# First MLP on token tiles of 512, 512, 256 and 512 that cross batch ends, in place of four batches of 448

## The chip, the cores and the metric

The kernel runs on one core of one Trainium2 chip. A core has five engines that work side by side, each on its own in-order stream of instructions: TensorE (PE in the profile; its weight loads are listed apart as PEld), VectorE (DVE), ScalarE (ACT), GpSimd (POOL) and SyncE (SP, which here only issues DMAs). The metric is the device time of one execution in microseconds (us), the median of several runs. TensorE's granted clock has two levels, 1.2 and 2.4 GHz; the profile gives it as a share of the upper one.

## The reference

Four batches of 448 tokens go through attention (12 heads of 64, RMS norm on q and k), a ReLU MLP with a LayerNorm and a residual, and a gated MLP whose gate mixes the tokens of a batch. All is fp32.

```python
q_n, k_n = rmsnorm(q, g_q), rmsnorm(k, g_k)                 # (4, 12, 448, 64)
attn = softmax(q_n @ k_n.T / sqrt(64)) @ v
x = attn.transpose(0, 2, 1, 3).reshape(4, 448, 768)
xn = (x - mean(x)) / sqrt(var(x) + 1e-6) * g_ln             # the first MLP
x = x + maximum(xn @ w_ch1, 0) @ w_ch2                      # 768 -> 3072 -> 768
h = maximum(x @ w_in, 0)                                    # the gated MLP, 768 -> 1024
u, v = h[..., :512], h[..., 512:]
v_s = einsum('ts,bsd->btd', w_spatial, layernorm(v)) + b_spatial[None, :, None]
out = (u * v_s) @ w_out                                     # 512 -> 768
```

The first MLP works on each token by itself: nothing in it asks where a batch ends. The attention before it and the gate behind it work batch by batch.

## The kernel before

Activations lie transposed: 128 model or hidden columns on the partitions, tokens along the free axis. Products in the MLPs are done as three matmuls (`THREE`) over parts of the operands, a high part and the remainder (hi and lo), so each activation tile is written twice, once by ACT (hi) and once by DVE (lo).

The first MLP takes the 3072 hidden columns in 24 units `u` of 128. For a unit and a batch `b` there are two groups of 18 matmuls, each 128x128 weights against 448 tokens: `ph` (L663, 6 blocks of the 768 model columns by 3) makes the hidden tile, ACT (L673) and DVE (L678) turn it into `h` hi and lo, and `pm` (L686, 6 output blocks by 3) multiplies by the second weight. DVE adds each of the 6 outputs into the residual `y` (L693). That is 24 x 4 x 36 = 3,456 matmuls of 448 tokens. The group order (`plan_groups`) is `ph` of one (u, b), then `pm` of the one before. `ph` tiles rotate over 2 PSUM banks, so a `ph` group waits until DVE has read the `ph` two groups earlier; `pm` tiles rotate over 3 and 3.

Weights stream in for each unit. DVE converts each piece of them, `wc`, in four operations (L92 to L95), ACT (L101) and POOL (L171) split it into `ws`.

The kernel is a list of steps with a cost, an engine and a due number `n` (`op`), and `arrange` orders each stage's steps greedily by those and emits every engine's stream in that order. Stages that matter here:

- A: attention over 24 pairs of heads, its outputs `x` transposed by PE (`pxT`, L541) and copied into `y` by ACT (L101), one copy per pair; the LayerNorm of batches 0, 1 and 2 as far as `lnx`; the hidden and output groups of unit 0 on batch 0, put in between.
- B, the transition: the rest of units 0 and 1. Beside it run the LayerNorm of batch 3 (a chain of short DVE operations to `lnab`, a broadcast by 8 small PE transposes `pbc`, L590, then on POOL a multiply L618 and an add L621 for each of 6 blocks, `lnx`), the `xn` tiles of batches 2 and 3 (ACT L635, DVE L638, 6 blocks each) and the conversion of the weight pieces for units 1 to 3.
- C: units 2 to 23. Then the gated MLP, batch by batch (`gv` L743, `gu` L806, `gs` L827, `gp` L874). Batch 0 takes its `y` from SBUF; batches 1 to 3 were stored to `y_dram` at the end of C (L1094, three DMAs on ACT's queue) and are loaded again; SP's small loads of the gate's bias `br` (L1124) and of `wout_r` (L1153) stand in the same stage as they.

Of the kernel before, what the change touches and what calls it, by code (L numbers as in the profile page):

```python
# [39 lines left out]
def attention_mlp_gated(ctx, tc, q, k, v, g_q, g_k, g_ln, w1, w2, w_in, w_sp, b_sp, w_out, out):  # L40
# [630 lines left out]
    def h_act(u, b, pl, tag):  # L671
        hs = pl.tile([P, 2, S], F32R, tag=tag, name=f"h{u}_{b}")
        nc.scalar.activation(hs[:, 0, :], hid[u, b][0][:, :S], AF.Relu)  # L673
        hid[u, b].append(hs)

    def h_dve(u, b):
        ph, hs = hid[u, b]
# [4 lines left out]
    def o_pe(u, b, m, pl):
        s2, hs = wsp["w2", u], hid[u, b][1]
        po = bank(pl, f"pm{u}_{b}_{m}")
        for e, (a, c) in enumerate(THREE):
# [3 lines left out]
        hid[u, b, m] = po

    def o_dve(u, b, m):
        po = hid.pop((u, b, m))
        nc.vector.tensor_tensor(y[b][:, m, :], po[:, :S], y[b][:, m, :], op=ALU.add)  # L693

    def plan_hidden(u, b, n, after=()):

        o, w1r = f"{u}_{b}", f"w1_{u}"
        pl, hs = ("s", "h0") if after else ("h", "hs")
# [7 lines left out]
        tiles = lambda: (ap["h0"], "h0") if after else (hpool, "h")  # L706
        op(n, "ACT", 0.424, lambda: h_act(u, b, *tiles()), r=["h" + o], w=["hs" + o], new=hs)
        op(n, "DVE", 0.535, lambda: h_dve(u, b), r=["h" + o], w=["hs" + o])

    def plan_outputs(u, b, n, pls):  # L710

        o = f"{u}_{b}"
# [503 lines left out]
```

## Times and profile before

| | us |
|---|---|
| median of 3 runs | 1281.92 (1281.67 to 1282.04) |
| the profiled execution | 1280.78 |
| its span, first to last instruction | 1278.9 |
| PE busy | 1238.7 (97%) |
| DVE busy | 908.3 (71%) |
| ACT busy | 456.1 (36%) |
| POOL busy | 335.8 (26%) |

The granted clock over the span is 0.996. The span is read in four parts: attention up to about 350 us, the transition B to about 415, units 2 to 23 to 1050, the gated MLP from there. "Busy" counts the time in which an engine has an instruction in work; a wait of an in-order engine appears as idle time in front of the instruction that waited, with the instruction that released it.

### The profile page before, as it was taken

Reading aid. Unit: us, or ns where it says so; the run is one execution under the profiler, and the core shown is the slowest. Engines: PE = TensorE matmul, PEld = TensorE weight load, DVE = VectorE, ACT = ScalarE, POOL = GpSimd, SP = SyncE. Lnnn points to the kernel's source line nnn. Section 1 sums busy time; section 2 is a strip of 40 time slices with the busy share of each in tenths; the row PEclk is TensorE's granted clock in tenths of the full one; section 3 lists DMA queues with packets and bytes.
Section 4 is the critical chain, followed back from the end, with each engine's and each line's share of the span. In section 5 each row is a group of like instructions: output and inputs, shape, how many; then the busy total and the mean of one; then the engine's idle time right before and its main releaser. Section 6 shows DMA issues by size and latency. Waiting matters only on the chain.

```text
span 1278.9 us, 16910 instructions
## 1 busy us (share of the span) xinstructions
PE 1238.7 (97%) x6528; PEld 1018.7 (80%) x6528; DVE 908.3 (71%) x1682; ACT 456.1 (36%) x910; POOL 335.8 (26%) x278
## 2 busy tenths in 40 slices
PE   4999999999899999999999999999999999999998
PEld 2555555555589999999999999999999998889998
DVE  7777787876598898787887888777776577543240
ACT  4777887878341222112222121121111123122212
POOL 5654866615061111111111111111111024221110
PEclk9999999999999999999999999999999999999999
DMA  4212211211021432222222233221110044111103
GB/s 101 73 51 62 62 44 44 76 40 42 10 98 40 132 106 93 91 75 85 89 75 83 87 101 108 77 73 50 50 50 25 1 150 178 44 44 38 50 1 87
DMA packets 50863, 89.01 MB, mean 70 GB/s; under 512 B 3952, under 2 KB 39152, under 8 KB 50016
## 3 DMA queue, kind: packets, MB, share of 16 engines
q1 hardware_dynamic: 50352, 83.82, 21.2%
q10 hardware_dynamic: 432, 4.13, 0.8%
q8 instruction: 51, 0.84, 0.3%
q14 instruction: 28, 0.23, 0.1%
HBM read 73.58 MB, written 14.35 MB: 69 GB/s over the span
## 4 chain that ended last, share of the span: by engine, by line
PE 85%; DVE 7%; ACT 3%; DMA 2%; POOL 2%; issue 1%; SPq 0%; ACTq 0%; DVEq 0%
PE ph L663 27%; PE pm L686 26%; PE po L486 5%; PE t L469 5%; PE s L438 5%; PE gp L874 5%; PE gv L743 4%; PE gu L806 3%; PE gs L827 3%; DVE nmx L444 2%; DMA win_ru<-win_dram 1%; ACT PT L101 1%; ACT P L450 1%; PE px L520 1%; DVE PT L479 1%
## 5 line engine op out<-in xcount | busy, mean ns | idle before, releaser
L693 DVE TENSOR_TENSOR y<-pm,y 128x448 f32<-128x448 f32 x576 | 320.4, 614 | 111.9 <-PE pm L686 111.9
L686 PE MATMUL pm<-h,ws 128*128 128x448 f32 x1728 | 369.4, 368 | 3.3 <-DVE y L693 2.5
L663 PE MATMUL ph<-xn,ws 128*128 128x448 f32 x1728 | 366.1, 365 | 0.0
L686 PEld LDWEIGHTS pm<-h,ws 128*128 128x128 f32 x1728 | 326.2, 189 | 31.5 <-issue 3.5
L663 PEld LDWEIGHTS ph<-xn,ws 128*128 128x128 f32 x1728 | 324.3, 188 | 26.0
L171 POOL TENSOR_TENSOR ws<-wc,ws 128x768 fp32r<-128x768 f32 x48 | 89.5, 1865 | 574.4 <-ACT ws L101 518.4
L673 ACT ACTIVATE h<-ph 128x448 fp32r<-128x448 f32 x96 | 52.1, 542 | 343.3 <-PE ph L663 336.1
L444 DVE TENSOR_REDUCE nmx<-s 112x2 f32<-112x896 f32 x96 | 104.2, 1086 | 43.4 <-PE s L438 42.5
L450 ACT ACTIVATE P<-s,nmx 112x448 f32<-112x448 f32 x192 | 121.3, 640 | 19.8 <-DVE nmx L444 16.3
L469 PEld LDWEIGHTS t<-ident,P 112*112 112x112 f32 x768 | 74.3, 133 | 42.3 <-ACT PT L101 20.5
L469 PE MATMUL t<-ident,P 112*112 112x112 f32 x768 | 92.8, 264 | 12.0 <-ACT PT L101 7.0
L438 PE MATMUL s<-kT,qT 64*112 64x448 f32 x384 | 98.0, 589 | 2.7 <-ACT P L450 1.9
L91 ACT ACTIVATE wc<-wr 128x768 f32<-128x768 f32 (+1 forms) x64 | 54.7, 859 | 85.7 <-DMA win_dram<-wc 42.4
L101 ACT ACTIVATE ws<-wc 128x768 fp32r<-128x768 f32 x48 | 40.6, 846 | 111.9 <-DVE wc L95 57.4
L486 PE MATMUL po<-PT,vr 112*64 112x448 f32 x384 | 79.2, 555 | 0.0
L101 ACT ACTIVATE PT<-t 112x896 f32<-112x896 f32 x72 | 65.9, 916 | 19.1 <-PE t L469 18.9
L678 DVE SCALAR_TENSOR_TENSOR h<-ph,h 128x448 fp32r<-128x448 f32 x96 | 59.2, 617 | 14.4 <-ACT h L673 14.4
L743 PE MATMUL gv<-winv,ys 128*112 128x512 f32 x288 | 67.2, 392 | 0.0
L743 PEld LDWEIGHTS gv<-winv,ys 128*112 128x112 f32 x288 | 50.1, 174 | 15.8
L94 DVE SCALAR_TENSOR_TENSOR wc<-wr,wc 128x768 int32<-128x768 int32 (+1 forms) x64 | 59.7, 935 | 1.5
L95 DVE SCALAR_TENSOR_TENSOR wc<-wr,wc 128x768 uint32<-128x768 uint32 (+1 forms) x64 | 60.0, 951 | 0.5
L874 PE MATMUL gp<-wout,gg 128*128 128x384 f32 x336 | 58.6, 334 | 0.0
(165 smaller groups left out, 1195.7 us busy)
## 6 DMA issues: line engine op xcount, KB each, us to landing
wr<-in_moe_w_ch_dram SPq DMA_DIRECT2D x48, 768.0 KB, 4.5
wr<-in_moe_w_in_dram SPq DMA_DIRECT2D x12, 512.0 KB, 3.7
vr<-in_v_dram SPq DMA_DIRECT2D x24, 224.0 KB, 2.7
kr<-in_k_dram SPq DMA_DIRECT2D x11, 448.0 KB, 4.0
qr<-in_q_dram SPq DMA_DIRECT2D x11, 448.0 KB, 4.7
y_dram<-y ACTq DMA_DIRECT2D x3, 1344.0 KB, 9.3
yl<-y_dram SPq DMA_DIRECT2D x3, 1344.0 KB, 5.6
win_dram<-wc SPq DMA_DIRECT2D x12, 256.0 KB, 5.5
```

Of the source, the lines that this page charges most:

```text
L101: nc.scalar.activation(d, s, AF.Copy)
L171: nc.gpsimd.tensor_tensor(t[:, 1], pl["c"], f32(t[:, 0]), op=ALU.subtract)
L438: nc.tensor.matmul(p[:CP, j, :S], pr["qT"][rows, c * CP : (c + 1) * CP], pr["kT"][rows], start=True, stop=True)
L444: nc.vector.tensor_reduce(t, pr["s", c][:CP, :, :S], axis=AX.X, op=ALU.max, negate=True)
L450: nc.scalar.activation(t, pr["s", c][:CP, j, :S], AF.Exp, bias=pr["m", c][:, j : j + 1], scale=1.0, accum_out=pr["sum"][:, j, c : c + 1],)
L469: nc.tensor.transpose(p[:CP, e, c * CP : (c + 1) * CP], pr["P", j, c][:, kc * CP : (kc + 1) * CP], ident[:CP, :CP])
L486: nc.tensor.matmul(pr["po"][j * D : (j + 1) * D, :S], raw["v", i][:, j, kc, :], pr["PT", kc // 2, j][:, kc % 2], start=(kc == 0), stop=(kc ...
L663: nc.tensor.matmul(hid[u, b][0][:, :S], s1[:, a, kk, :], xn[b][:, c, kk, :], start=(kk == 0 and m == 0), stop=(kk == NK - 1 and m == 2),)
L686: nc.tensor.matmul(po[:, :S], s2[:, a, m * P : (m + 1) * P], hs[:, c, :], start=(e == 0), stop=(e == 2))
L693: nc.vector.tensor_tensor(y[b][:, m, :], po[:, :S], y[b][:, m, :], op=ALU.add)
L743: nc.tensor.matmul(pv[:CP, :], ys[b][:, a, kk, c * CP : (c + 1) * CP], W["v", kk][:, e], start=(kk == 0 and m == 0), stop=(kk == NK - 1 an ...
L874: nc.tensor.matmul(po[:, :half_n], gt[g][:, a, i * P : (i + 1) * P], W["out", g][:, e, half * half_n : (half + 1) * half_n], start=(g == 0 ...
```

## The change

The tokens of all four batches, 1792 in a row, are cut into tiles of 512, 512, 256 and 512. `y`, `xn` and the groups of the first MLP go by tile `t` (a group is named by unit, tile and first column), so a unit has the same 144 matmuls on tiles of four sizes. What is made by batch is written in pieces: `pieces_of(b)` gives one piece for batch 0 (tile 0, 448 tokens), two for batch 1 (64 of tile 0, 384 of tile 1), three for batch 2 (128 of tile 1, 256 of tile 2, 64 of tile 3), one for batch 3 (448 of tile 3). The copies into `y`, the multiply of `lnx` and both parts of `xn` are done piece by piece: 18 more of each.

In the transition tile 1 of unit 0 is done in two groups, the 384 tokens of batch 1 early and the 128 of batch 2 late, so there are 3,456 + 36 matmuls in all. The planner's costs follow the number of tokens. The pools `OT` and `x` of the attention have one buffer in place of two, `y_dram` is laid out by model column and stored by tile (tile 0 gives its last 64 tokens), and two tiles of the gated MLP lie in other pools.

```diff
-    y_dram = dram.tile([B, P, NK, S], F32, name="y_dram")
+    y_dram = dram.tile([P, NK, B * S], F32, name="y_dram")
...
+    TILES = ((0, 512), (512, 512), (1024, 256), (1280, 512))
+    SEGMENTS = tuple((t, 0, size) for t, (first, size) in enumerate(TILES))
+
+    def pieces_of(b):
+
+        parts = []
+        for t, (first, size) in enumerate(TILES):
+            lo, hi = max(first, b * S), min(first + size, (b + 1) * S)
+            if lo < hi:
+                parts.append((t, slice(lo - first, hi - first), slice(lo - b * S, hi - b * S)))
+        return parts
+
+    def batches_of(t, lo, hi):
+        first = TILES[t][0]
+        return range((first + lo) // S, (first + hi - 1) // S + 1)
...
+            for t, cols, own in pieces_of(b):
+                if t not in y:
+                    y[t] = y_a.tile([P, NK, TILES[t][1]], F32, tag=f"y{t}", name=f"y{t}")
+                act_copy(y[t][:, hp, cols], pr["pxT"][:, own])
...
-                nc.gpsimd.tensor_tensor(t, y[b][:, m], ln["bc"][:, 0], op=ALU.mult)
+                for e, cols, own in pieces_of(b):
+                    nc.gpsimd.tensor_tensor(t[:, own], y[e][:, m, cols], ln["bc"][:, 0, own], op=ALU.mult)
...
-    def plan_xn(b, xn_pool, n, step):
+    def plan_xn(b, n, step):
...
-                xn[b] = xn_pool.tile([P, 2, NK, S], F32R, tag="xn", name=f"xn{b}")
-            nc.scalar.activation(xn[b][:, 0, m, :], ln["x", m], AF.Copy, scale=gl_c[:, m : m + 1])
+            for t, cols, own in pieces_of(b):
+                if t not in xn:
+                    tag = "xn" if t < 2 else f"xn{t}"
+                    xn[t] = xn_pools[t].tile([P, 2, NK, TILES[t][1]], F32R, tag=tag, name=f"xn{t}")
+                nc.scalar.activation(xn[t][:, 0, m, cols], ln["x", m][:, own], AF.Copy, scale=gl_c[:, m : m + 1])
...
+            for t, cols, own in pieces_of(b):
+                nc.vector.scalar_tensor_tensor(
+                    xn[t][:, 1, m, cols], ln["x", m][:, own], gl_c[:, m : m + 1], f32(xn[t][:, 0, m, cols]),
+                    op0=ALU.mult, op1=ALU.subtract,
+                )
...
+        o, w1r, k = f"{u}_{t}_{lo}", f"w1_{u}", (hi - lo + 40) / 488
+        pl, hs = ("s", "PT") if after else ("h", "hs")
...
+            xr = [f"xn{b}_{m}" for b in batches_of(*s) for m in kks]
             op(
-                n, "PE", 0.56 * step, lambda kks=kks: h_pe(u, b, kks, pl),
-                r=[w1r, *after] + [f"xn{b}_{m}" for m in kks], w=["h" + o], new=None if kk else pl,
+                n, "PE", 0.61 * k * step, lambda kks=kks: h_pe(u, s, kks, pl),
+                r=[w1r, *after] + xr, w=["h" + o], new=None if kk else pl,
...
-            ("qkT", 2), ("P", 14), ("PT", 5), ("OT", 2), ("x", 2),
+            ("qkT", 2), ("P", 14), ("PT", 5), ("OT", 1), ("x", 1),
...
-        plan_hidden(0, 0, n + 4, ["done"])
+        plan_hidden(0, SEGMENTS[0], n + 4, ["done"])
...
-        plan_xn(2, xn_c, 0, 3)
+        plan_xn(2, 0, 3)
         plan_norm_x(3, 0, 3)
-        plan_xn(3, xn_c, 16, 3)
-        plan_groups(((0, 1), (1, 0), (1, 1), (0, 2), (1, 2), (0, 3), (1, 3)), 0)
+        plan_xn(3, 16, 3)
+        early, late = (1, 0, 2 * S - TILES[1][0]), (1, 2 * S - TILES[1][0], TILES[1][1])
+        s0, s1, s2, s3 = SEGMENTS
+        plan_groups(((0, early), (1, s0), (1, s1), (0, late), (0, s2), (1, s2), (0, s3), (1, s3)), 0)
...
-            plan_groups([(u, b) for b in range(B)], n)
+            plan_groups([(u, s) for s in SEGMENTS], n)
...
-        for b in range(1, B):
+        plan_ys(0, lambda: y[0][:, :, :S], 14, 1)
+        for t, (first, size) in enumerate(TILES):
+            cols = slice(0 if t else S, size)
             op(
-                7 * b + 14, "SPA", 0.6, lambda b=b: nc.scalar.dma_start(y_dram[b], y[b]),
-                r=[f"y{b}_{m}" for m in range(NK)], w=[f"yd{b}"],
+                7 * t + 14, "SPA", 0.6,
+                lambda t=t, cols=cols, first=first: nc.scalar.dma_start(
+                    y_dram[:, :, first + cols.start : first + cols.stop], y[t][:, :, cols]
+                ),
+                r=[f"y{b}_{t}_{m}" for b in batches_of(*SEGMENTS[t]) if b or t for m in range(NK)], w=[f"yd{t}"],
...
-        gp = {"vs": xn_b}
-
-        for nm, n in (("g", 4), ("o", 2), ("u", 4), ("t", 2), ("w", 1), ("vr", 4), ("small", 2)):
+        gp = {}
+
+        for nm, n in (("g", 4), ("o", 2), ("u", 4), ("t", 2), ("vs", 1), ("vr", 4), ("small", 2)):
...
-            nc.sync.dma_start(yl[b], y_dram[b])
+            nc.sync.dma_start(yl[b], y_dram[:, :, b * S : (b + 1) * S])
```

How that moves the streams is seen best in the transition. On PE, before, the broadcast of batch 3's LayerNorm (`pbc3`) stands behind unit 1's hidden group on batch 1 (`ph1_1`); the suffixes are unit, batch, and for `pm` the output block.

```order
L663 MATMUL ph1_0_4053<-xn0_1639,ws2_4010 128x448 x18
...
L663 MATMUL ph1_1_4119<-xn1_2591,ws2_4010 128x448 x18
L590 MATMUL pbc3_0_4150<-ident_63,lnab3_4037 128x112 x4
...
L686 MATMUL pm1_0_0_4166<-h1_0_4091,ws3_4141 128x448 x3
...
L686 MATMUL pm1_1_0_4205<-h1_1_4156,ws3_4141 128x448 x3
...
L663 MATMUL ph0_2_4248<-xn2_4040,ws0_3564 128x448 x18
```

After it, PE's stream at that place; suffixes are unit, tile, first column, and for `pm` the output block.

```order
L689 MATMUL ph1_0_0_4110<-xn0_1637,ws2_4054 128x512 x18
...
L610 MATMUL pbc3_0_4191<-ident_63,lnab3_4081 128x112 x4
...
L715 MATMUL pm1_0_0_0_4205<-h1_0_0_4156,ws3_4175 128x512 x3
...
L689 MATMUL ph1_1_0_4273<-xn1_2603,ws2_4054 128x512 x18
L689 MATMUL ph0_1_384_4307<-xn1_2603,ws0_3607 128x128 x18
L689 MATMUL ph0_2_0_4338<-xn2_4085,ws0_3607 128x256 x18
...
L715 MATMUL pm1_1_0_0_4360<-h1_1_0_4328,ws3_4175 128x512 x3
```

The broadcast now stands ahead of unit 1's hidden group on the second tile, and that group, which takes 128 tokens of batch 2, behind the output group `pm1_0`; the three tiles that follow have 512, 128 and 256 tokens.

On DVE, before, one operation per block writes `xn` of batch 2 (`lnx2_5` is its sixth and last block), and only unit 0's group on batch 2 needs it; `xn3` is batch 3's, `wc5` a weight piece.

```order
L693 TENSOR_TENSOR y0_576<-pm1_0_5_4198,y0_576 128x448
L92 TENSOR_SCALAR wc5_4177<-wc5_4177 128x768
L638 SCALAR_TENSOR_TENSOR xn2_4040<-lnx2_5_3603,gl_c_70,xn2_4040 128x448
L93 TENSOR_SCALAR wc5_4177<-wc5_4177 128x768
L638 SCALAR_TENSOR_TENSOR xn3_4218<-lnx3_0_4179,gl_c_70,xn3_4218 128x448
```

After it, DVE's stream from the pieces of the fifth block to those of the sixth (the three pieces of the fourth stand right ahead).

```order
L92 TENSOR_SCALAR wc4_4146<-wc4_4146 128x512
L662 SCALAR_TENSOR_TENSOR xn1_2603<-lnx2_4_3603,gl_c_70,xn1_2603 128x128
L662 SCALAR_TENSOR_TENSOR xn2_4085<-lnx2_4_3603,gl_c_70,xn2_4085 128x256
L662 SCALAR_TENSOR_TENSOR xn3_4087<-lnx2_4_3603,gl_c_70,xn3_4087 128x64
L93 TENSOR_SCALAR wc4_4146<-wc4_4146 128x512
L723 TENSOR_TENSOR y0_573<-pm1_0_0_0_4205,y0_573 128x512
L94 SCALAR_TENSOR_TENSOR wc4_4146<-wr4_4101,wc4_4146 128x512
...
L723 TENSOR_TENSOR y0_573<-pm1_0_0_5_4243,y0_573 128x512
L92 TENSOR_SCALAR wc5_4222<-wc5_4222 128x768
L662 SCALAR_TENSOR_TENSOR xn1_2603<-lnx2_5_3646,gl_c_70,xn1_2603 128x128
```

The last piece that unit 1's group on tile 1 reads, `xn1` of block 5, now stands behind the conversion of `wc4`, six adds and the first step of `wc5`, all in the one stream.

## Rows read from the trace of the kernel before

**Rows 1.** The page, part 1: busy time, share of the span, instructions.

```profile
PE 1238.7 (97%) x6528; PEld 1018.7 (80%) x6528; DVE 908.3 (71%) x1682; ACT 456.1 (36%) x910; POOL 335.8 (26%) x278
```

**Rows 2.** Windows: stretch, length, busy PE, PEld, DVE, ACT, POOL, clock, DMA share, GB/s.

```profile
0.00:350.00 350.00, 317.62 (x1982) 174.09 (x1983) 261.55 (x563) 250.45 (x578) 176.82 (x182) 1.00 0.21 55
...
380.00:395.00 15.00, 12.25 (x47) 10.43 (x46) 15.00 (x26) 2.39 (x4) 5.07 (x3) 0.77 0.11 35
...
500.00:600.00 100.00, 100.00 (x495) 92.67 (x494) 79.09 (x139) 22.05 (x32) 12.94 (x7) 1.00 0.27 88
```

**Rows 3.** Timeline of PE, steady units: start, us, line, operation [idle before <-releaser].

```profile
503.02 3.81 PE L686 MATMUL pm<-h,ws 128*128 128x448 f32 x18
...
524.91 3.81 PE L686 MATMUL pm<-h,ws 128*128 128x448 f32 x18
```

**Rows 4.** Timeline of PE in the gated MLP.

```profile
1094.46 16.71 PE L743 MATMUL gv<-winv,ys 128*112 128x512 f32 x72
1111.01 14.56 PE L806 MATMUL gu<-ys,winu 128*128 128x448 f32 x72
1125.41 9.87 PE L827 MATMUL gs<-wsp_s,gvs 112*128 112x448 f32 x48
...
1166.13 29.31 PE L874 MATMUL gp<-wout,gg 128*128 128x384 f32 x168
```

**Rows 5.** Groups by form: line, engine, operation, count, busy us, mean ns, idle before.

```profile
L101 ACT ACTIVATE PT<-t 112x896 f32<-112x896 f32 x72 | 65.9, 916 | 19.1 <-PE t L469 18.9
...
L874 PEld LDWEIGHTS gp<-wout,gg 128*128 128x128 f32 x336 | 58.3, 188 | 0.1
...
L101 ACT ACTIVATE OT<-po 128x448 f32<-128x448 f32 x24 | 13.0, 543 | 31.2 <-PE po L486 31.2
```

**Rows 6.** Timeline of PE in the transition.

```profile
349.60 7.68 PE L663 MATMUL ph<-xn,ws 128*128 128x448 f32 x36
...
360.83 3.88 PE L663 MATMUL ph<-xn,ws 128*128 128x448 f32 x18
364.55 0.93 PE L590 MATMUL pbc<-ident,lnab 112*128 112x112 f32 x8
...
372.86 7.60 PE L663 MATMUL ph<-xn,ws 128*128 128x448 f32 x36
382.95 0.71 PE L686 MATMUL pm<-h,ws 128*128 128x448 f32 x1 [2.49 <-DVE y L693]
383.92 9.82 PE L686 MATMUL pm<-h,ws 128*128 128x448 f32 x35 [0.26 <-DVE h L678]
...
400.88 3.81 PE L686 MATMUL pm<-h,ws 128*128 128x448 f32 x18
```

**Rows 7.** Timeline of DVE in the transition.

```profile
357.45 0.96 DVE L94 SCALAR_TENSOR_TENSOR wc<-wr,wc 128x768 int32<-128x768 int32 x1
...
359.93 0.15 DVE L583 SCALAR_TENSOR_TENSOR lnab<-lnmv,lnab 112x4 f32<-112x4 f32 x1
360.00 3.27 DVE L693 TENSOR_TENSOR y<-pm,y 128x448 f32<-128x448 f32 x6
...
371.66 1.08 DVE L92 TENSOR_SCALAR wc<-wc 128x768 f32<-128x768 f32 x1
...
377.07 1.90 DVE L94 SCALAR_TENSOR_TENSOR wc<-wr,wc 128x768 int32<-128x768 int32 x1
...
382.19 1.14 DVE L693 TENSOR_TENSOR y<-pm,y 128x448 f32<-128x448 f32 x2
```

**Rows 8.** Timeline of POOL in the same stretch.

```profile
379.95 3.32 POOL L621 TENSOR_TENSOR lnx<-lnx,lnbc 128x448 f32<-128x448 f32 x2
```

**Rows 9.** Timeline of PE in the attention: small matmuls with a weight load each.

```profile
152.21 0.98 PE L469 MATMUL t<-ident,P 112*112 112x112 f32 x8 [0.18 <-ACT PT L101]
153.03 0.55 PE L541 MATMUL pxT<-ident,x 112*128 112x112 f32 x4
```

**Rows 10.** The stores of `y`, L1094: time from issue to landing.

```profile
DMA to landing us min/median/max: 6.7/9.3/10.7
```

More of the change, by code (lines that the diff above doesn't have):

```diff
@@ L557, in plan_pair @@
         op(m + 1, "PE", 0.38, xT_pe, r=[f"x{i}"], w=[f"pxT{i}"], new="x")
-        op(m + 1, "ACT", 0.55, xT_act, r=[f"pxT{i}"], w=[f"y{b}_{hp}"])
+        w = [f"y{b}_{t}_{hp}" for t, _, _ in pieces_of(b)]
+        op(m + 1, "ACT", 0.3 + 0.25 * len(w), xT_act, r=[f"pxT{i}"], w=w)
     lnst = {}
@@ L669, in h_pe, with h_act, h_dve, o_pe @@
                 )
[L671 to L677, printed above, removed]
+    def h_act(u, s, pl, tag):
+        t, lo, hi = s
+        hs = pl.tile([P, 2, 512], F32R, tag=tag, name=f"h{u}_{t}_{lo}")
+        nc.scalar.activation(hs[:, 0, : hi - lo], hid[u, s][0][:, : hi - lo], AF.Relu)
+        hid[u, s].append(hs)
+    def h_dve(u, s):
+        n = s[2] - s[1]
+        ph, hs = hid[u, s]
         nc.vector.scalar_tensor_tensor(
-            hs[:, 1, :], ph[:, :S], 0.0, f32(hs[:, 0, :]), op0=ALU.max, op1=ALU.subtract
+            hs[:, 1, :n], ph[:, :n], 0.0, f32(hs[:, 0, :n]), op0=ALU.max, op1=ALU.subtract
         )
-    def o_pe(u, b, m, pl):
-        s2, hs = wsp["w2", u], hid[u, b][1]
-        po = bank(pl, f"pm{u}_{b}_{m}")
+    def o_pe(u, s, m, pl):
+        t, lo, hi = s
+        s2, hs = wsp["w2", u], hid[u, s][1]
+        po = bank(pl, f"pm{u}_{t}_{lo}_{m}")
         for e, (a, c) in enumerate(THREE):
             nc.tensor.matmul(
-                po[:, :S], s2[:, a, m * P : (m + 1) * P], hs[:, c, :], start=(e == 0), stop=(e == 2)
+                po[:, : hi - lo], s2[:, a, m * P : (m + 1) * P], hs[:, c, : hi - lo], start=(e == 0), stop=(e == 2)
             )
[L689 to L698, printed above, removed]
+        hid[u, s, m] = po
+    def o_dve(u, s, m):
+        t, lo, hi = s
+        po = hid.pop((u, s, m))
+        nc.vector.tensor_tensor(y[t][:, m, lo:hi], po[:, : hi - lo], y[t][:, m, lo:hi], op=ALU.add)
+    def plan_hidden(u, s, n, after=()):
+        t, lo, hi = s
+        o, w1r, k = f"{u}_{t}_{lo}", f"w1_{u}", (hi - lo + 40) / 488
+        pl, hs = ("s", "PT") if after else ("h", "hs")
         step = 1 if after else NK
@@ L701, in plan_hidden, with plan_outputs @@
             kks = range(kk, kk + step)
+            xr = [f"xn{b}_{m}" for b in batches_of(*s) for m in kks]
             op(
-                n, "PE", 0.56 * step, lambda kks=kks: h_pe(u, b, kks, pl),
-                r=[w1r, *after] + [f"xn{b}_{m}" for m in kks], w=["h" + o], new=None if kk else pl,
-            )
[L706 to L712, printed above, removed]
+                n, "PE", 0.61 * k * step, lambda kks=kks: h_pe(u, s, kks, pl),
+                r=[w1r, *after] + xr, w=["h" + o], new=None if kk else pl,
+            )
+        tiles = lambda: (ap["PT"], "PT") if after else (hpool, "h")
+        op(n, "ACT", 0.54 * k, lambda: h_act(u, s, *tiles()), r=["h" + o], w=["hs" + o], new=hs)
+        op(n, "DVE", 0.6 * k, lambda: h_dve(u, s), r=["h" + o], w=["hs" + o])
+    def plan_outputs(u, s, n, pls):
+        t, lo, hi = s
+        o, k = f"{u}_{t}_{lo}", (hi - lo + 40) / 488
         for m in range(NK):
             pl = pls[m]
-            op(n, "PE", 0.56, lambda m=m, pl=pl: o_pe(u, b, m, pl), r=["hs" + o, f"w2_{u}"], w=[f"po{o}_{m}"], new=pl)
-            op(n, "DVE", 0.535, lambda m=m: o_dve(u, b, m), r=[f"po{o}_{m}"], w=[f"y{b}_{m}"])
+            op(n, "PE", 0.61 * k, lambda m=m, pl=pl: o_pe(u, s, m, pl), r=["hs" + o, f"w2_{u}"], w=[f"po{o}_{m}"], new=pl)
+            w = [f"y{b}_{t}_{m}" for b in batches_of(*s)]
+            op(n, "DVE", 0.6 * k, lambda m=m: o_dve(u, s, m), r=[f"po{o}_{m}"], w=w)
     def plan_groups(groups, n):
-        for u, b in groups:
-            plan_hidden(u, b, n)
+        for u, s in groups:
+            plan_hidden(u, s, n)
             if todo[0]:
                 plan_outputs(*todo[0], n, "ooommm")
-            todo[0] = (u, b)
+            todo[0] = (u, s)
             n += 7
@@ L1155, in wout_hi @@
         def wout_hi(g):
-            W["out", g] = gp["w"].tile([P, 2, DM], F32R, name=f"wout{g}")
+            if g == 0:
+                W["out"] = xn_b.tile([P, NG, 2, DM], F32R, tag="xn", name="wout")
+            W["out", g] = W["out"][:, g]
             nc.vector.tensor_copy(W["out", g][:, 0], st["wr", g])
```

39 lines of the change are left out of this document (16 added, 23 removed).

## The prediction, written before the changed kernel ran

> **What bounds the kernel now.** I read the page's busy times first: PE works 1238.7 us of the span, 97%, DVE 71% [rows 1]. The windows then show where the missing 3% lies. From 500 to 600 us PE is busy throughout and DVE 79% [rows 2], so the steady units cost what their matmuls cost. A timeline of PE there gives that price: from the first to the last `pm` shown lie six groups of 18, 21.89 us or 202.7 ns a matmul [rows 3]. At 2.4 GHz, the upper level, 448 columns are 186.7 ns; 16.0 ns come on top. The transition is the other place: in 380 to 395 us PE was busy 12.25 of 15 us, DVE all 15, and the clock was 0.77 [rows 2]. PE's timeline shows the stop: 2.49 us before 382.95, for DVE's adds [rows 6].
>
> From 349.60, the first hidden group behind the attention, to 400.88, the output group of unit 0 on its last batch, are 51.28 us [rows 6]. The work in it is 12 groups of 18 at 3.65 us and 0.93 for the broadcast, 44.7. So 6.6 us were lost there: the stop, and matmuls at the lower clock behind it (35 of them took from 383.92 for 9.82 us, where 7.1 would do).
>
> **The change part by part.** All sums stand against the profiled execution's 1280.78 us; the median shown is 1.1 above it, added at the end.
>
> *Steady groups.* The columns are the same; a unit's groups of 448 become 512, 512, 256, 512. If a matmul costs columns/2.4 + 16.0 ns, 144 matmuls of a unit cost the same in both. Other rows give the extra as 13.3 ns (`gu`, 448 columns, 14.40 us for 72), 14.5 (`gp`, 384, 29.31 for 168), 16.5 (`gv`, 512, 16.55 for 72) [rows 4], and 20.0 (3.72 us for the 18 at 360.83) [rows 6]. 0, with bounds 3,492 x (-2.7) = -9.4 and 3,492 x 4.0 = +14.0. DVE adds of 448 come every 0.53 us (six in 3.27, the next at once) [rows 7]; for all sizes together the columns are the same, so DVE's 79% stays.
>
> *The split of tile 1 in unit 0.* 36 more matmuls. Of 128 columns each would cost 53 + 16 = 69 ns, but the nearest small ones, 112 columns with a weight load each, come every 0.10 us (8 in 0.82) [rows 9]. Merged, the 128 columns would cost 53 ns: 36 x 47 ns = +1.7, with bounds 0.6 (16 ns each) and 5.4 (a full 202.7 ns each). Here a rule of the Trainium skill speaks against the change. The rows show weight loads of 188 ns [rows 5] below matmuls that come every 174.5 ns [rows 4], so load and matmul run side by side. "TensorE: Matmul & The Clock Gate", section "The mechanism", says that loads overlap matmuls in flight only when the row group differs; and section "LDWEIGHTS (loading the stationary operand)" prices 128 columns at 107 ns. By that the 36 would cost, as an estimate, 36 x (107 + 16) = 4.4 us. The trace disagrees with the first, and I stay with 1.7.
>
> *The transition.* I follow PE's new order at 2.4 GHz and 16 ns: 18 matmuls are 3.2 us for 384 columns, 4.1 for 512, 2.2 for 256, 1.8 for the late 128. From 349.60: `ph0` early to 352.8, `ph1` on tile 0 to 356.9, `pm0` early to 360.1. The broadcast now stands here, where DVE's short chain has only just ended (359.93 before [rows 7], some 0.6 later with six more pieces of `xn` in it at about 0.1): 0.6 us lost. It is done at 361.6, `pm1` on tile 0 at 365.7, and the group `ph1` on tile 1 runs to its 17th matmul, 369.4. That one needs the last `xn1` piece, which now stands behind the six adds of `pm1`.
>
> When does DVE get there? Its adds of `pm0` begin at about 360.7 and end at 363.5 (six of 0.47). Then 12 operations with both operands in SBUF: six pieces of `xn`, the steps of `wc4` and the first of `wc5`, and the piece itself. Alone, with 0.96 for the 768 columns of L94 [rows 7] and less for fewer, they are about 4.4 us, and six adds of 512 are 3.7: 371.6, a wait of 2.2. But POOL's 12 operations for batch 3's `lnx` begin as soon as the broadcast is through, some 362.5, where before they began with it at 365; they take 1.66 us each here [rows 8], to 382. And beside them DVE's operations grow: L94 is 0.96 without and 1.90 with POOL [rows 7], 0.94 more, and the seven operations from 371.66 to 382.19 took 10.53 us, 1.50 each [rows 7]. I take the 0.94 for the eight that stand in one run and none for the four between adds: 379.1, a wait of 9.7 us. If all 12 pay, 3.8 more.
>
> What a small piece pays is the second place for a rule. The row has a long operation that pays 0.94. The Trainium skill, "SBUF — State Buffer", "Who interferes with whom", calls the port that DVE and GpSimd share an exclusive lock, held for a whole instruction. By it a piece of 64 columns waits as long as one of 448, as I have it. If instead the two shared bandwidth, each operation would grow by its own length (1.90/0.96), the eight by 2.3 us in place of 7.5, and the total below would be 5.2 lower. No row has a small operation beside POOL; the seven rows at 1.50 for lengths from 0.5 to 0.96 fit the lock better.
>
> From 379.1 PE finishes `ph1` (0.5) and runs the late 128 columns (1.8). Then `ph0` on tile 2 needs the bank of `ph1`, which DVE frees only by `h1` on tile 1, ten operations on: 5.9 us alone, 0.6 for `h1` itself, two more waits on POOL: 387.5. That is 6.1 us lost, and the lower clock behind the stop falls mostly within it (the 0.77 of 15 us before is 6.9 us at 1.2 GHz, rest included [rows 2]); 0.4 for the rest. New losses 0.6 + 9.7 + 6.1 + 0.4 = 16.8; the old 6.6 go: **+10.2**. Bounds: -6.6 with no stop at all, and +14.0 with all 12.
>
> *Tile 0 in the attention.* Its unit 0 group has 64 tokens more there and the transition 64 fewer: 0. Attention's own additions are 18 copies and 6 pieces of `xn` on ACT; by OT at 448 elements and PT at 896 [rows 5] a copy's fixed part is 2 x 543 - 916 = 170 ns, so 4.1 us of ACT, which is busy 250 of 350 us [rows 2]. Idle time of ACT covers them where PE does not wait on it; +1, bounds 0 and 4.1. The single buffers of `OT` and `x` cost nothing: the next pair's use is one pair, 350/24 = 14.6 us, later.
>
> *The gate's start.* The last store of `y` took up to 10.7 us to land [rows 10], and SP's loads of the bias and `wout_r` come behind it. It carries 512 tokens in place of 448: 12.2, so 1.5 late, and runs are shorter. DVE and `gs` come behind these loads: +1, bounds 0 and 3.
>
> Sum: 0 + 1.7 + 10.2 + 0 + 1 + 1 = 13.9, 1294.7 profiled, **1296** as the median.
>
> **The rivals.**
> 1. *The pieces come in time* and there is no stop (the other side). The place is the last `xn1` piece; it decides if DVE reaches it by 369.4, which it misses by 2.2 us even without POOL, or if the wait is short enough that the clock stays up. For: the adds read PSUM and may not wait for POOL, and the order leaves POOL's first operations waiting for `lnx` buffers. Against: DVE was full from 365 to 395. Then -6.6 + 1.7 + 2 = -2.9: 1279.0.
> 2. *The extra per matmul falls* to the 13.3 of `gu`, as fewer groups change hands at 512: 13.9 - 9.4 = +4.5, 1286. For: the rows differ by form. Against: `gv`, with 512 columns, has 16.5.
> 3. *It rises* to the 20.0 of the transition: +27.9, 1310.
> 4. *256 columns are bound by the weight load.* Loads of 188 ns [rows 5] under matmuls of 123: if a load overlaps no more than one matmul, 24 x 36 matmuls cost 65 ns more each, +56: 1352. For: loads stay at 188 in rows where the matmul is shorter. Against: small matmuls with loads every 0.10 us [rows 9]. The rule on overlap named above would also end on this side.
>
> **How the numbers follow.** Forecast 0.54, its own range 1286 to 1306 (bounds of the transition's waits, the split and the ends); rival 1 0.20, rival 2 0.13, rival 3 0.06, rival 4 0.07. The range of 1278 to 1309 leaves out the lower third of rival 1, half of rival 3 and rival 4. A measurement of this kernel can tell 0.2%, 2.6 us, from no change: faster is below 1279.4, slower above 1284.5. Rival 1 lies at the first edge: 0.13 faster, 0.05 same, and with a little from rival 2 the chances are 0.15, 0.10 and 0.75.
>
> **What the profile would show.** Matmuls of 512, 256 and 128 columns every 229, 123 and 100 ns in the steady units and the late group; before `ph1`'s last matmuls in the transition an idle time of some 10 us with releaser DVE `xn`, and before `ph0` on tile 2 a second; the clock well below 1 in 370 to 395; pieces of `xn` on DVE of 1 us and more. I am wrong if PE runs through there, or if 256 columns take much over 123 ns.

## The result, and the profile after

The changed kernel takes 1292.38 us (median of 16 runs, 1289.07 to 1295.73), the one before 1281.8 (16 runs, 1279.02 to 1293.38): a ratio on record of 1.0057, 95% interval 1.003 to 1.0084 (the two medians alone stand at 1.0083). It is slower, by 10.6 us of median, at 1296 forecast. The runs before lie in two groups, twelve at 1279 to 1283 us and four at 1291 to 1293.4; the last section has what sets them apart. The profiled execution before (1280.78) is of the lower group, the one after took 1293.51.

The page after, its first part and the clock in 40 slices; these lines answer to [rows 1].

```profile
span 1291.5 us, 17103 instructions
PE 1238.0 (96%) x6564; PEld 967.8 (75%) x6564; DVE 926.5 (72%) x1707; ACT 460.0 (36%) x947; POOL 334.9 (26%) x296
...
PEclk9999999999987999999999999999999999999999
```

PE is busy as long as before, and the clock falls in the 12th and 13th slice, 355 to 420 us. Cut at the same amounts of work left, the two spans are:

| stretch | before, us | after, us | difference | forecast |
|---|---|---|---|---|
| to the first transposes of `k` | 13.02 | 14.03 | +1.0 | 0 |
| attention, to the first `ph` of the transition | 336.58 | 342.00 | +5.4 | +1 |
| from there, until the columns of 22 units are left | 58.57 | 73.56 | +15.0 | +11.9 |
| those 22 units, to the first `gv` | 642.05 | 635.01 | -7.0 | 0 |
| the gated MLP | 228.70 | 226.88 | -1.8 | +1 |
| span | 1278.9 | 1291.5 | +12.6 | +13.9 |

The transition after has 110,592 columns of matmuls, the one before 112,896: tile 0 takes 64 tokens more of unit 0 into the attention. At 2.4 GHz these 2,304 columns are 1.0 us, so for the same work the transition lost 16.0 us and the attention 4.4.

PE's timeline in the transition after (start, length, operation, idle before and its releaser); before it is [rows 6].

```profile
356.03 7.46 PE L689 MATMUL ph<-xn,ws 128*128 128x384 f32 x36
363.32 3.31 PE L715 MATMUL pm<-h,ws 128*128 128x384 f32 x18
367.88 0.60 PE L610 MATMUL pbc<-ident,lnab 112*128 112x112 f32 x4 [1.25 <-DVE y L723]
369.92 0.60 PE L610 MATMUL pbc<-ident,lnab 112*128 112x112 f32 x4 [1.43 <-DVE y L723]
370.28 5.97 PE L715 MATMUL pm<-h,ws 128*128 128x512 f32 x18
376.09 3.79 PE L689 MATMUL ph<-xn,ws 128*128 128x512 f32 x16
385.36 4.95 PE L689 MATMUL ph<-xn,ws 128*128 128x512 f32 x20 [5.48 <-DVE xn L662]
395.93 4.21 PE L689 MATMUL ph<-xn,ws 128*128 128x256 f32 x18 [5.62 <-DVE h L706]
399.94 6.93 PE L715 MATMUL pm<-h,ws 128*128 128x512 f32 x36
...
421.43 4.24 PE L715 MATMUL pm<-h,ws 128*128 128x512 f32 x18
```

The group on tile 1 stops behind its 16th matmul, for an `xn` piece, and tile 2's group stops for `h`, which frees its bank. The broadcast waits twice as well, for the adds that free its banks; the second of these waits is for an add that stands behind the last step of the LayerNorm chain, `lnab`. Four stops are 13.8 us. Windows of the same stretch (busy PE, PEld, DVE, ACT, POOL, then the clock):

```profile
380.00:395.00 15.00, 4.95 (x20) 4.57 (x20) 15.00 (x20) 3.53 (x6) 7.01 (x5) 0.65 0.33 104
386.00:400.00 14.00, 8.38 (x39) 8.10 (x38) 12.69 (x14) 3.53 (x6) 6.55 (x4) 0.50 0.18 63
395.00:410.00 15.00, 14.07 (x82) 13.17 (x83) 10.78 (x23) 0.77 (x2) 0.00 (x0) 0.79 0.04 11
```

PE works a third of 380 to 395 us, DVE all of it, and the clock is still low behind it. DVE's timeline there, as [rows 7] before:

```profile
367.75 1.64 DVE L603 SCALAR_TENSOR_TENSOR lnab<-lnmv,lnab 112x4 f32<-112x4 f32 x1
...
371.64 3.57 DVE L662 SCALAR_TENSOR_TENSOR xn<-lnx,gl_c,xn 128x128 fp32r<-128x128 f32 x3
375.14 0.41 DVE L92 TENSOR_SCALAR wc<-wc 128x512 f32<-128x512 f32 x1
375.47 3.63 DVE L662 SCALAR_TENSOR_TENSOR xn<-lnx,gl_c,xn 128x128 fp32r<-128x128 f32 x3
379.02 0.42 DVE L93 TENSOR_SCALAR wc<-wc 128x512 int32<-128x512 int32 x1
...
384.97 0.93 DVE L662 SCALAR_TENSOR_TENSOR xn<-lnx,gl_c,xn 128x128 fp32r<-128x128 f32 x3
```

Three pieces (128, 256 and 64 tokens) take 3.57 us while GpSimd works on `lnx`, and 0.93 us at 384.97, when it is idle (it waits from 380.4 to 386). One by one, the pieces of 64, 128 and 256 tokens take 1.18, 1.19 and 1.36 us beside GpSimd and 0.27, 0.34 and 0.47 alone: 0.9 us more each, whatever the length. `lnab`, four columns wide, took 1.64 us beside GpSimd's

```profile
367.57 1.80 POOL L189 TENSOR_TENSOR ws<-wc,ws 128x768 fp32r<-128x768 f32 x1 [8.08 <-ACT ws L101]
```

where before it took 0.15 [rows 7]. The adds, which read PSUM, do not wait: 0.68 us for 512 columns at 379.36 with GpSimd at work, 0.67 at 382.71 with GpSimd idle. The steady units, as [rows 3]:

```profile
510.38 2.32 PE L715 MATMUL pm<-h,ws 128*128 128x256 f32 x18
512.53 4.27 PE L689 MATMUL ph<-xn,ws 128*128 128x512 f32 x18
516.63 4.24 PE L715 MATMUL pm<-h,ws 128*128 128x512 f32 x18
520.72 4.24 PE L689 MATMUL ph<-xn,ws 128*128 128x512 f32 x18
...
528.88 2.31 PE L689 MATMUL ph<-xn,ws 128*128 128x256 f32 x18
531.03 4.27 PE L715 MATMUL pm<-h,ws 128*128 128x512 f32 x18
```

A matmul of 512 columns costs 4.09/18 = 227 ns, 13 over columns/2.4, one of 256 costs 2.15/18 = 119, again 13 over; the 448 before had 16.0 over. The group of 512 right behind one of 256 takes a little more: 228.2 ns a matmul over the units, the other two 226.7, so 512 columns cost 227.2 in the mean.

### The profile page after: what moved, and what is told of

Read it like the earlier page. It is cut to its first block, busy times and chain, and to the rows that moved or that the text cites. A ratio compares the mean times of both kernels' runs of the same rounds, so it can differ in the third digit from the quotient of the medians.

```text
span 1291.5 us, 17103 instructions
## 1 busy us (share of the span) xinstructions
PE 1238.0 (96%) x6564; PEld 967.8 (75%) x6564; DVE 926.5 (72%) x1707; ACT 460.0 (36%) x947; POOL 334.9 (26%) x296
## 4 chain that ended last, share of the span: by engine, by line
PE 82%; DVE 9%; ACT 4%; DMA 2%; issue 1%; POOL 0%; SPq 0%; ACTq 0%; DVEq 0%; POOLq 0%
PE pm L715 24%; PE ph L689 23%; PE po L504 6%; PE t L487 5%; PE gv L777 5%; PE s L456 5%; PE gp L908 5%; PE gu L840 4%; PE gs L861 3%; DVE y L723 2%; ACT PT L101 2%; DVE nmx L462 1%; ACT P L468 1%; DVE xn L662 1%; DVE wc L94 1%
## 5 line engine op out<-in xcount | busy, mean ns | idle before, releaser
L723 DVE TENSOR_TENSOR y<-pm,y 128x512 f32<-128x512 f32 (+2 forms) x582 | 324.5, 610 | 97.5 <-PE pm L715 97.0
L689 PE MATMUL ph<-xn,ws 128*128 128x512 f32 (+3 forms) x1746 | 367.4, 365 | 11.1 <-DVE h L706 5.6
L715 PE MATMUL pm<-h,ws 128*128 128x512 f32 (+3 forms) x1746 | 365.8, 363 | 0.7 <-DVE PT L497 0.5
L689 PEld LDWEIGHTS ph<-xn,ws 128*128 128x128 f32 x1746 | 302.0, 192 | 62.0 <-DVE xn L662 5.9
L715 PEld LDWEIGHTS pm<-h,ws 128*128 128x128 f32 x1746 | 300.0, 190 | 52.9 <-issue 1.2
L700 ACT ACTIVATE h<-ph 128x512 fp32r<-128x512 f32 (+2 forms) x97 | 52.0, 536 | 232.9 <-PE ph L689 232.6
L706 DVE SCALAR_TENSOR_TENSOR h<-ph,h 128x512 fp32r<-128x512 f32 (+2 forms) x97 | 59.2, 611 | 14.4 <-ACT h L700 14.4
L92 DVE TENSOR_SCALAR wc<-wc 128x768 f32<-128x768 f32 (+1 forms) x64 | 42.9, 671 | 31.6 <-ACT wc L91 31.5
L95 DVE SCALAR_TENSOR_TENSOR wc<-wr,wc 128x768 uint32<-128x768 uint32 (+1 forms) x64 | 64.1, 1007 | 0.3
```

Of the source, the lines that this page charges most:

```text
L689: nc.tensor.matmul(hid[u, s][0][:, : hi - lo], s1[:, a, kk, :], xn[t][:, c, kk, lo:hi], start=(kk == 0 and m == 0), stop=(kk == NK - 1 and ...
L715: nc.tensor.matmul(po[:, : hi - lo], s2[:, a, m * P : (m + 1) * P], hs[:, c, : hi - lo], start=(e == 0), stop=(e == 2))
L723: nc.vector.tensor_tensor(y[t][:, m, lo:hi], po[:, : hi - lo], y[t][:, m, lo:hi], op=ALU.add)
```

## The experiments

Theory: the transition is lost to DVE operations that have all their operands in SBUF, each of which waits for a whole GpSimd operation, with PE's next operand or bank behind them in DVE's one stream. (The texts put down ahead of the runs speak of two SBUF operands. But the conversion step L93, which reads one, also took 1.50 us beside GpSimd in the kernel before, at 374.15, and 0.56 alone.) Rivals: DVE simply has too much work of its own there; or the loss lies elsewhere (buffers, layout). The steady gain and the attention's loss were open. Ratios are to the kernel before, run on the same chip, both of its groups together; the medians of the lower group alone are 1280.0 to 1280.8 us there. In each case "attention" and "transition" are the stretches of the table above.

**One buffer for OT and x, in the kernel before.**

```diff
-            ("qkT", 2), ("P", 14), ("PT", 5), ("OT", 2), ("x", 2),
+            ("qkT", 2), ("P", 14), ("PT", 5), ("OT", 1), ("x", 1),
...
```

(The planner's count of these buffers goes down with them.)

> The kernel before, with one buffer in place of two for the attention's OT and x tiles and nothing else. In the changed kernel the first hidden group of the transition starts at 356.03 us in place of 349.60, 6.4 later. Theory 'buffers': PE waits for tiles that are still being read, so here that group starts at 353 to 356 and the whole is 1285 to 1288. Rival 'pieces' (the cut copies into y, the cut xn pieces and the wider group of unit 0 shift the order in the attention): start within 1.5 us of 349.6, whole 1281 to 1283. Everything behind the attention keeps its length in both.

1280.05 us, ratio 1.0011 (0.9968 to 1.0053). The attention stretch is 335.3 us, the transition starts at 348.14. 'Buffers' is refuted.

**Four tiles of 448 in the changed kernel.**

```diff
-    TILES = ((0, 512), (512, 512), (1024, 256), (1280, 512))
+    TILES = ((0, 448), (448, 448), (896, 448), (1344, 448))
...
-        plan_groups(((0, early), (1, s0), (1, s1), (0, late), (0, s2), (1, s2), (0, s3), (1, s3)), 0)
+        plan_groups(((0, s1), (1, s0), (1, s1), (0, s2), (1, s2), (0, s3), (1, s3)), 0)
...
```

> The changed kernel with four tiles of 448 (no pieces, no split of tile 1), but with its pools, its planner costs and its layout of y_dram; the xn tile of batch 1 has a stride of 512 columns, the other xn tiles and the hidden tiles 448. Attention: 'buffers' says that the transition starts at 353 to 356, 'pieces' 349 to 351. Transition: 51 to 53 us to unit 0's output group on the last batch, as before, in place of 65, in every theory. Steady units: 'size' (448 columns cost 16.0 ns over columns/2.4, 512 and 256 cost 13.3) says 202.7 ns a matmul in all groups; 'stride' says 200.0 in the hidden groups of batch 1 and 202.7 in the rest; 'schedule' (the new costs and pools do it) says 200.0 everywhere. Whole: 1281 to 1283 with 'pieces' and 'size', 1285 to 1288 with 'buffers' and 'size', 8 less with 'schedule'.

1283.73 us, ratio 1.0044 (1.0001 to 1.0088). Attention 337.1, so neither the pools nor the matmul groups' new costs make it long (nothing is written in pieces here, so the costs of pieces are not tried); transition 59.4. The steady units are a surprise; PE's timeline of its profiled execution:

```profile
701.29 3.88 PE L715 MATMUL pm<-h,ws 128*128 128x448 f32 x18
705.01 3.88 PE L689 MATMUL ph<-xn,ws 128*128 128x448 f32 x18
708.73 3.88 PE L715 MATMUL pm<-h,ws 128*128 128x448 f32 x18
```

3.72 us a group, 206.7 ns a matmul, 20.0 over, in every group of that execution, the tile with the wider stride included. 'Stride' and 'schedule' fall. 'Size' had the price lower, at 202.7: 448 columns cost more than 16.0 over here, in the same groups that had 16.0 in the kernel before.

**Batch 3's LayerNorm later, in the changed kernel.**

```diff
-        plan_ln(3, 0, "o")
+        plan_ln(3, 12, "o")
...
-        plan_norm_x(3, 0, 3)
-        plan_xn(3, 16, 3)
+        plan_norm_x(3, 20, 3)
+        plan_xn(3, 24, 3)
```

> The changed kernel with the LayerNorm of batch 3 planned later, so that its broadcast stands behind unit 1's hidden group on tile 1 and GpSimd's twelve lnx operations begin behind the xn pieces that this group needs. Theory 'lock' (each DVE operation with two SBUF operands waits for a whole GpSimd operation beside it): a piece takes 0.31 us in place of 1.17, the eight DVE operations ahead of pm1's adds take 2.5 us in place of 7.7, and PE's stop inside that group falls from 5.5 us to under 1; some of it comes back as a later wait for xn3, whole 1282 to 1288. Rival 'DVE's own work' (there are simply too many operations ahead): pieces stay near 1 us each, the stop stays at 4 to 6, whole 1291 to 1294.

1282.26 us, ratio 0.9984 (0.9948 to 1.002). Tile 1's group on PE, the pieces of block 5 on DVE that it waits for, and GpSimd, which begins `lnx` only at 385.12:

```profile
377.46 4.25 PE L689 MATMUL ph<-xn,ws 128*128 128x512 f32 x18
```
```profile
378.88 0.94 DVE L662 SCALAR_TENSOR_TENSOR xn<-lnx,gl_c,xn 128x128 fp32r<-128x128 f32 x3
```
```profile
385.12 3.67 POOL L639 TENSOR_TENSOR lnx<-y,lnbc 128x448 f32<-128x448 f32 x2
```

Same instructions, GpSimd away: the three pieces take 0.94 us and the stop of 5.48 is gone. 'Lock' holds, "DVE's own work" does not. Other stops came (2.25, 1.17, 1.59 us), and the transition took 64.5, 9.1 less than in the changed kernel.

**Tile 1's pieces first**, with costs by size for the pieces.

```diff
-        plan_xn(2, 0, 3)
+        plan_xn(2, 0, 0, (1,))
+        plan_xn(2, 8, 1, (2, 3))
...
+            us = sum(0.15 + 0.0012 * (own.stop - own.start) for _, _, own in pieces())
...
```

> The changed kernel with batch 2's xn pieces for tile 1 (six of 128 tokens) planned ahead of its pieces for tiles 2 and 3, and unit 1's hidden group on tile 1 then ahead of the broadcast. Theory (the stop comes from one late piece in DVE's stream, and the stops and the half clock behind them are what the transition lost): no stop in that group, the transition takes 50 to 55 us in place of 65, the whole is 1279 to 1284, about as long as before. Rival (the same DVE work is due in the same stretch, so the wait only moves to the groups on tiles 2 and 3): transition 60 to 65, whole 1288 to 1292.

1277.92 us, ratio 0.9962 (0.9932 to 0.9992), 2.1 us under the median of the lower group: as fast as forecast by the theory and a little more. But the transition took 61.5, not the theory's 50 to 55: that is the rival's number (60 to 65), and the wait did in part move to the next group. What is left, on PE:

```profile
364.16 4.28 PE L694 MATMUL ph<-xn,ws 128*128 128x512 f32 x18
...
373.44 2.12 PE L694 MATMUL ph<-xn,ws 128*128 128x128 f32 x18
381.55 5.94 PE L720 MATMUL pm<-h,ws 128*128 128x512 f32 x18 [5.98 <-DVE y L728]
```

Tile 1's group runs through; the next stop is for adds, which need no GpSimd but stand in DVE's stream behind eight operations beside it, six pieces and two conversion steps, from 370.00 to 380.22. The attention is 340.0 here, 2.0 shorter than in the changed kernel, and nothing else in the edit touches that stage but the corrected costs; the three kernels below that have them take 339.7 to 339.9.

**The pieces alone, in the kernel before** (every line that writes `y`, `lnx` or `xn` of a batch does so in slices).

```diff
+    CUTS = ((0, 448), (0, 64, 448), (0, 128, 384, 448), (0, 448))
...
-            act_copy(y[b][:, hp, :], pr["pxT"][:, :S])
+            for own in cuts(b):
+                act_copy(y[b][:, hp, own], pr["pxT"][:, own])
...
```

> The kernel before with four tiles of 448 as they were, and only the writing in pieces added: the copies into y, the multiply of lnx and both parts of xn are cut at 64 of 448 for batch 1 and at 128 and 384 for batch 2, 18 more instructions of each kind; sizes of matmuls, order and costs stay. From the first transposes of q and k to the first hidden group of the transition the kernel before takes 336.6 us, the changed one 342.0, the one with four tiles of 448 337.1. Theory 'pieces': the cut operations alone make that stretch 340 to 342. Rival 'width' (the group of 512 in the attention and the order that it gives): 336.5 to 337.5. In the transition, 'lock' says that only the pieces of batch 2's last two blocks meet GpSimd, four more operations of 0.9 us, so 58.6 becomes 60 to 63; if pieces cost only their own length there, 58.5 to 59.5.

1284.52 us, ratio 1.0008 (0.9967 to 1.0049). The attention is 339.5 us, 2.9 of the 5.4: between the two expectations, so both have a part. The transition is 58.8, the number of the side that gave pieces their own length only; 'lock' had 60 to 63. The pieces beside GpSimd do take three times as long, as the row shows, but what that cost PE is small: it stopped 2.63 and 0.60 us for the adds behind them, where before it stopped 2.49 and 0.26 [rows 6].

```profile
368.22 2.77 DVE L647 SCALAR_TENSOR_TENSOR xn<-lnx,gl_c,xn 128x128 fp32r<-128x128 f32 x3
```

**All pieces of batch 2 ahead.**

```diff
-        plan_xn(2, 0, 0, (1,))
-        plan_xn(2, 8, 1, (2, 3))
+        plan_xn(2, -2, 0, (1,))
+        plan_xn(2, -1, 0, (2, 3))
```

> As the kernel that writes batch 2's pieces for tile 1 first, but its pieces for tiles 2 and 3 follow at once too, ahead of the LayerNorm chain of batch 3, so that all 18 run before GpSimd begins with lnx. There the stop of 5.98 us was for y adds that stood behind eight pieces beside GpSimd. Theory: pieces take 0.3 us each, that stop falls to 0 to 2 us, the transition takes 55 to 59 us in place of 61.5, the whole is 1272 to 1276. Rival (the later wc and xn3 operations pay the same waits, in the same stretch): 60 to 62, whole 1277 to 1279.

A miss on both sides: 1291.2 us, ratio 1.0039 (1.0005 to 1.0073), transition 75.3. The pieces took 0.3 us each, but PE made three long stops for `h`, the operation that frees a `ph` bank:

```profile
363.92 6.40 PE L694 MATMUL ph<-xn,ws 128*128 128x512 f32 x18 [4.62 <-DVE h L711]
...
386.44 4.21 PE L694 MATMUL ph<-xn,ws 128*128 128x256 f32 x18 [4.01 <-DVE h L711]
...
396.90 8.01 PE L720 MATMUL pm<-h,ws 128*128 128x512 f32 x29 [5.83 <-DVE h L711]
```

The new order runs unit 0's late group at once, which takes the second `ph` bank, and sets `h` behind the pieces, a weight conversion and, later, operations beside GpSimd. The pieces were short here and the stops long: what stands ahead of the bank-freeing operation counts, not the pieces as such.

**Three other sizes.**

```diff
-    TILES = ((0, 512), (512, 512), (1024, 256), (1280, 512))
+    TILES = ((0, 480), (480, 480), (960, 448), (1408, 384))
...
```

> The changed kernel with tiles of 480, 480, 448 and 384 tokens, to read the price of a matmul by its columns in the steady units. In four traces 448 columns cost 202.7 ns (twice) or 206.7 ns (twice), over the whole first MLP of a run, 512 and 256 always 226.7 and 119.4. 'Size': 448 again has 202.7 or 206.7, and 480 and 384 have extras of their own between 13.3 and 20. 'Rest of 512' (only sizes that divide a bank evenly are free of it): 480, 448 and 384 all have 16 or 20 over columns/2.4. 'Length of the matmul' (the extra comes where a matmul is about as long as its weight load of 188 ns): 480 (200 ns) and 384 (160 ns) have 13.3, 448 (187 ns) alone has 16 or 20. Whole: 1290 to 1305, the transition being laid out worse.

1300.98 us (two runs), ratio 1.0111 (1.0026 to 1.0196). The steady groups, twice:

```profile
505.25 3.81 PE L715 MATMUL pm<-h,ws 128*128 128x448 f32 x18
508.90 4.08 PE L689 MATMUL ph<-xn,ws 128*128 128x480 f32 x18
...
724.84 4.07 PE L715 MATMUL pm<-h,ws 128*128 128x480 f32 x18
728.74 3.88 PE L689 MATMUL ph<-xn,ws 128*128 128x448 f32 x18
732.46 4.06 PE L715 MATMUL pm<-h,ws 128*128 128x480 f32 x18
736.36 3.29 PE L689 MATMUL ph<-xn,ws 128*128 128x384 f32 x18
739.49 0.77 PE L715 MATMUL pm<-h,ws 128*128 128x448 f32 x3
```

480 costs 3.90/18 = 216.7 ns (16.7 over), 384 3.13/18 = 173.9 (13.9 over). 448 has both prices within one execution: 206.7 (20.0 over) in every `ph` group between 430 and 1045 us, as at 728.74, and 203.0 (16.3 over) in every `pm` group, as at 505.25. 384 has 173.7 in `ph` and 175.2 in `pm`. Of the three expectations only 'size' is not against this, and it does not say enough: of the five sizes seen in the first MLP, 256, 384 and 512 pay 13 to 15 over columns/2.4, 448 and 480 pay 16 to 20, and the kind of group matters too.

**Adds before pieces**, on top of tile 1's pieces first, with and without a later LayerNorm of batch 3.

```diff
-        plan_ln(3, 0, "o")
+        plan_ln(3, 6, "o")
...
-        plan_xn(2, 8, 1, (2, 3))
-        plan_norm_x(3, 0, 3)
-        plan_xn(3, 16, 3)
+        plan_xn(2, 15, 1, (2, 3))
+        plan_norm_x(3, 14, 3)
+        plan_xn(3, 24, 3)
```

(The later LayerNorm is three numbers: its chain by 6, its `lnx` by 14, its `xn` by 8.)

> The kernel with tile 1's pieces first, and two due numbers moved: batch 2's pieces for tiles 2 and 3 from 8 to 15, so that in DVE's stream the adds of pm1 on tile 0 and h1 on tile 1 stand ahead of ten of them, and batch 3's LayerNorm by 6, so that the broadcast stands behind that pm1. Theory (the stops are DVE operations that free PSUM banks, standing behind pieces beside GpSimd): the stop of 5.98 us before pm1 on tile 1 goes, one of 1 to 4 us comes before unit 0's group on tile 2 or 3; the transition takes 55 to 59 us in place of 61.5, whole 1272 to 1276. Rival (the sum of DVE's and GpSimd's work between the broadcast and xn of batch 3 sets the end, whatever the order): 60 to 64, whole 1277 to 1281.

1275.46 us, ratio 0.9941 (0.9911 to 0.9971): the fastest, ahead of both kernels, and 5.4 us under the median of the lower group. The whole is as the theory said, the transition (60.5) as the rival said: the stops are short now, three of 2.30, 1.36 and 0.77 us, but some clock is still lost.

```profile
374.59 4.37 PE L720 MATMUL pm<-h,ws 128*128 128x512 f32 x18
378.79 2.07 PE L694 MATMUL ph<-xn,ws 128*128 128x256 f32 x16
383.17 0.50 PE L694 MATMUL ph<-xn,ws 128*128 128x256 f32 x2 [2.30 <-DVE xn L665]
385.03 1.54 PE L720 MATMUL pm<-h,ws 128*128 128x128 f32 x6 [1.36 <-DVE y L728]
```

The second moves the pieces alone:

```diff
-        plan_xn(2, 8, 1, (2, 3))
+        plan_xn(2, 15, 1, (2, 3))
```

> The same without moving batch 3's LayerNorm: only batch 2's pieces for tiles 2 and 3 are due later. GpSimd begins as early as with tile 1's pieces first, the adds of pm1 stand ahead of the pieces. Theory: the stop before pm1 on tile 1 shrinks to 0 to 2 us, a stop of 2 to 5 us comes before unit 0's group on tile 2, whose last piece stands behind nine operations beside GpSimd; the transition takes 56 to 60 us, whole 1273 to 1277. Rival: 60 to 64, whole 1277 to 1281.

1278.73 us, ratio 0.995 (0.9921 to 0.9979), 2.1 us under the median of the lower group, transition 62.6: the rival's numbers. The stop before `pm1` on tile 1 is gone, stops of 0.47, 2.61 and 1.27 us inside tile 2's group and 1.17 behind it came in its place. The stops on PE add up to 5.5 us here, 6.7 with tile 1's pieces first and 4.4 with the later LayerNorm as well: this order of the adds mostly moved the stop, and taking GpSimd out of the way as well shortened it a little more.

## Why the prediction was right, and where it was not

**The transition** is the step that carried the sum, and its mechanism went as written: the 17th matmul of tile 1's group waits for the last `xn1` piece, and tile 2's group for `h`. The first stop is 5.48 us in place of 9.7, though the piece came when forecast: the prediction has it 29.5 us behind the first hidden group of the transition, it was there after 29.3. Two errors cancelled in that. The run of eight operations took 7.7 us where I had 9.8, since its six pieces paid 0.9 each as written and the two conversion steps nothing (GpSimd stood idle as they began). And the adds ahead of them ended 1.8 us later than written, chiefly because `lnab` took 1.64. What made the stop shorter is PE, which reached it after 23.8 us and not after 19.8: the broadcast lost 2.7, not 0.6, not by the length of the LayerNorm chain, which I named, but by its PSUM banks, which the adds of `pm0` free, with the long `lnab` among those adds; and `pm1` behind it took 5.8 us, not 4.1, at a clock of 0.50 from 372 to 374.

The second stop was put at 6.1 and is 5.62. And the lower clock was mis-sized: I let it fall within the stops and added 0.4. Behind them 18 matmuls of 256 columns took 4.01 us, where steady ones take 2.15; the clock was 0.50 from 386 to 400. At steady prices the work of the stretch is 52.4 us (110,592 columns at 2.4 GHz, 288 times 13.3 ns, some 1.6 for the late groups, 0.9 for the broadcast); 73.56 less that and less 13.8 of stops leaves 7.4 us, most of it the clock.

The exclusive lock that the Trainium skill states ("SBUF — State Buffer", "Who interferes with whom") agrees with the trace: pieces of 64 to 256 tokens cost 1.19 us each beside GpSimd and 0.31 without, and each pays 0.9 whatever its length. Growth by their own length would have given 0.6. The prediction says that no row has a small operation beside GpSimd. The trace before has one, which would have told the lock from shared bandwidth: four columns, beside a GpSimd operation that ran from 351.22 for 1.85 us, where an operation of this size takes 0.15 alone.

```profile
351.26 1.83 DVE L80 SCALAR_TENSOR_TENSOR lnt<-lnab 112x4 f32<-112x4 f32 x1
```

**The split** was put at 1.7 us. At full clock, with tile 1's pieces first, late matmuls of 128 columns come every 0.11 us, 36 x (111 - 53) = 2.1; in the changed kernel the 18 of `ph` ran at the lower clock.

**The steady groups** are the step that failed: "a matmul costs columns/2.4 + 16.0 ns" was read from one size and carried to others. 512 and 256 pay some 13 to 14: the 22 units are 2,376 matmuls at 227.2 and 792 at 119.6 ns, 634.5 us against the 642.05 before, -7.5, of which -7.0 was left. That is rival 2's term (-9.4), come true beside the forecast and not in its place; its reason, fewer hand-overs at 512, is not shown, since 256 pays no more. Rivals 1 and 4 fell: PE did stop, and 256 columns cost 119 ns.

**The attention** failed too: +5.4 against 1, above its bound of 4.1. I priced ACT's fixed part. The pieces alone make 2.9, the 2,304 columns moved into this stage up to 1.0, and corrected costs in the planner, with the same pieces, give 2.0 back; so about 2 is the order that wrong costs produced. How the 2.9 divide between ACT, DVE and GpSimd is not shown.

**The gate**: I had the last store land after 12.2 us; the four took 4.2 to 9.3, and the wait of 0.74 us inside `gs` went. -1.8 in place of +1. Five of the six profiles with these tiles have 226.8 to 226.9; with tile 1's pieces first it was 228.4, and there the 0.74 in `gs` is back. Why it comes and goes is open.

So 13.9 against 12.6 is partly luck: 4.4 too little for the attention, 3.1 for the transition and 1.0 for the first loads (12.6 to 14.6 us over all the profiles, without a known cause) stand against 7.0 too much for the steady units and 2.8 for the gate.

## What to carry to other kernels

When operations are cut into pieces, count what each piece waits for, not only its length: beside a busy GpSimd, DVE operations with all operands in SBUF each cost a full wait (0.9 us a piece here), and whatever frees a PSUM bank should stand ahead of them in the stream. Teach a planner the new costs with the new shapes. And read the price of a matmul at the size that will be used: a changed tile size can pay in the steady part and lose in the seams, and the seams can then be mended one at a time.
